# Leaving the next row out of the column steps of 32x32 triangular inverses, and doing it by itself

## The chip, the cores and the metric

The kernel runs on one core of one Trainium2 chip. The metric is the device time of one execution in microseconds (us), median of the runs. A core has several engines that each work through their own queue of instructions in order and wait for each other through semaphores: TensorE (PE in the profile; matrix products), VectorE (DVE), ScalarE (ACT), GpSimd (POOL), and SyncE (SP), which issues most of the DMA transfers.

## What is computed

Two blocks follow each other. The first is a delta-rule attention: for each of 4 x 8 heads, 768 tokens, head size 48, with normalised keys,

```
for t in range(S):
    y[t]  = q[t] @ state
    state = state + beta[t] * outer(k[t], v[t] - k[t] @ state)
```

The second sends each of the 3,072 resulting rows of 384 numbers to one of 16 experts (the best of 4 groups, then the best of 4 experts in it), each a two-layer network 384 -> 1024 -> 384 with a ReLU, scaled by the two gate probabilities. All is in fp32.

## The kernel before, in words

**Chunks.** The 768 tokens are cut into 24 chunks of C = 32. Within a chunk the recurrence is a triangular system: with the Gram matrix of the keys, a 32x32 unit lower triangular matrix per head is inverted, and then the whole chunk goes through TensorE. There are 128 partitions = 4 batches x 32 tokens, and after a transposition 128 partitions = 32 heads of four chunks; so one call of `inverse(g)` (lines 237 to 302) inverts the matrices of 4 chunks (RG = 4) at once, each partition holding a 32x32 matrix `m` of its own. Six such inverses serve the 24 chunks.

**An inverse.** `m` is transposed in from the Gram matrices `gt` (L243); a square root on ScalarE (L250) and some small VectorE operations give the norms and the scaling; two passes over 1,024 elements make `m` (L272) and `cs` (L277). Then come the column steps j = 1 .. 30. With n = 31 - j rows below row j, a step multiplies column j below row j by row j up to column j (`t`, n x j elements, L284) and adds the product to the block below row j (L288). Each of these operations reads what the one before it wrote. At the end come the product with `cs` (L290), the diagonal (L292), the transposition `mt` (L295) and, on ScalarE, two masked copies `mtb` (L300), which TensorE uses in the chunks.

**A chunk** (`advance(u)`, lines 315 to 370). TensorE brings in the scaled values `vh` (L321, made by VectorE at L308), subtracts what the state holds (L327) and starts the output (L336); ScalarE copies the result to `f`; TensorE applies the inverse (`w_ps`, L343); ScalarE copies to `w`; TensorE updates the state (`s_ps`, L353); ScalarE copies it to `s_bd` (L359), which the next chunk needs; TensorE finishes the output (L364). In between TensorE does the Gram products of a later chunk (`gram`, L225; ScalarE copies `gt`, VectorE masks `gq`, L233) and the router's logits of the chunk before (L385, L393; ScalarE's copy `lg`, L395).

**Routing** (`route(r)`, lines 398 to 497) takes the logits of four chunks: about 25 small VectorE operations find the group and the expert (`gb` L420 to `hots` L448), an exponential on ScalarE (L459), ranks `rk` from TensorE's `r_ps` (L462), `place` (L464), `mine` (L484); GpSimd compares (`at`, L489) and TensorE sorts (L495).

**The order** of TensorE, VectorE, ScalarE and GpSimd is written out by hand. VectorE's long tasks (inverses and routes) are generators that yield after each instruction, and a planner slips their instructions between the chunks' own: `work(n)` credits each running task with n x 180 x its share, and each instruction costs the task 180 plus the count of elements that it yields (`push`, line 507). Steps for ScalarE or TensorE wait for marked points in a chunk (`allow`). With `SHARE` = 0.9 the inverse of four chunks later is spread over about four chunks; inverse g starts when chunk 4(g-2)+2 ends, but its column steps do not begin before inverse g-1 is done.

**Then** the tokens are fetched by expert (GpSimd, L685) and the 16 experts run through TensorE (`hidden` L706, `second` L720), and results are scattered (L736).

Of the kernel before, what the change touches and what calls it, by code (L numbers as in the profile page):

```python
# [8 lines left out]
F32 = mybir.dt.float32  # L9
I32 = mybir.dt.int32  # L10
AX = mybir.AxisListType
ALU = mybir.AluOpType
# [3 lines left out]
C = 32  # L16
# [46 lines left out]
def deltanet_then_moe(  # L63
# [13 lines left out]
    nc = tc.nc  # L77
# [6 lines left out]
    NE, _, F = w1_d.shape  # L84
# [69 lines left out]
    with ExitStack() as first:  # L154
        ap_ = first.enter_context(tc.tile_pool(name="attn", bufs=1))
        wk = first.enter_context(tc.tile_pool(name="wk", bufs=2))
# [80 lines left out]
        def inverse(g):  # L237

            m = wk.tile([128, C, C], F32, tag="m", name=f"m{g}")
            flat = m.rearrange("p i j -> p (i j)")
            nc.vector.transpose(out=flat, in_=gts.pop(g).rearrange("p t u h -> p (t u h)"))  # L243
            yield C * C
            diag = flat[:, ::C + 1]
            nrm, r0, r1 = [sm.tile([128, C], F32, tag=n, name=f"{n}{g}")
                           for n in ("nrm", "r0", "r1")]
            nc.vector.tensor_tensor(r0, diag, cut["tiny"].to_broadcast([128, C]), op=ALU.max)
            yield ACT_STEP
            nc.scalar.activation(r0, r0, ACT.Sqrt)  # L250
            yield SOON
            nc.vector.reciprocal(r1, r0)
            yield
            nc.vector.tensor_tensor(r1, r1, diag, op=ALU.mult)
            yield
            nc.vector.tensor_tensor(r0, r0, r1, op=ALU.add)
            yield
            nc.vector.scalar_tensor_tensor(nrm, in0=r0, scalar=-0.5,
                                           in1=cut["eps"].to_broadcast([128, C]), op0=ALU.mult,
                                           op1=ALU.subtract)  # L260
            yield
            nc.vector.reciprocal(r1, nrm)
            yield
            nc.vector.tensor_tensor(r1, r1, r1, op=ALU.mult)
            yield
            nc.vector.scalar_tensor_tensor(r0, in0=r1, scalar=-1.0, in1=bt[:, g], op0=ALU.mult,
                                           op1=ALU.mult)
            yield
            norm[g] = sm.tile([128, C], F32, tag="normt", name=f"normt{g}")
            nc.vector.transpose(out=norm[g], in_=nrm)  # L270
            yield
            nc.vector.tensor_tensor(m, m, r0[:, :, None].to_broadcast([128, C, C]), op=ALU.mult)  # L272
            yield C * C
            while g and g - 1 not in mts:
                yield TURN
            cs = wk.tile([128, C, C], F32, tag="cs", name=f"cs{g}", bufs=1)
            nc.vector.tensor_tensor(cs, cut["below"].rearrange("p (i j) -> p i j", i=C),  # L277
                                    r0[:, None, :].to_broadcast([128, C, C]), op=ALU.mult)
            yield C * C
            for j in range(1, C - 1):  # L280
                n = C - 1 - j
                t = wk.tile([128, C * C // 4], F32, tag="t", name=f"t{g}_{j}")
                tv = t[:, 0:n * j].rearrange("p (i c) -> p i c", i=n)
                nc.vector.tensor_tensor(tv, m[:, j + 1:, j:j + 1].to_broadcast([128, n, j]),  # L284
                                        m[:, j:j + 1, 0:j].to_broadcast([128, n, j]),
                                        op=ALU.mult)
                yield n * j
                nc.vector.tensor_tensor(m[:, j + 1:, 0:j], m[:, j + 1:, 0:j], tv, op=ALU.add)  # L288
                yield n * j
            nc.vector.tensor_tensor(m, m, cs, op=ALU.mult)  # L290
            yield C * C
            nc.vector.tensor_scalar(diag, r0, -1.0, None, op0=ALU.mult)  # L292
            yield
            mt = wk.tile([128, RG * H, C], F32, tag="cs", name=f"mt{g}", bufs=1)
            nc.vector.transpose(out=mt.rearrange("p r i -> p i r"), in_=flat)  # L295
            mtb = wk.tile([128, RG * H, 2, C], F32, tag="mtb", name=f"mtb{g}")
            yield 2 * C * C
            yield ACT_STEP
            for a in range(2):
                nc.scalar.activation(mtb[:, :, a], mt, ACT.Copy,  # L300
                                     scale=cut["parity"][:, a:a + 1])
            mts[g] = mtb
# [198 lines left out]
        behind, held, rate, due = [], {}, {}, {}  # L501
# [5 lines left out]
        def push(task):  # L507
            said = next(task, "end")
            if said == "end":
                behind.remove(task)  # L510
                held.pop(task, None)
                allow(TURN)
            else:
                held[task] = said if isinstance(said, str) else None
                due[task] -= 180 + (said if isinstance(said, int) else 0)

        def work(n):


            for task in behind:  # L520
                due[task] = min(due[task] + n * 180 * rate[task], 4000.0)
            while True:
                able = [t for t in behind if held.get(t) is None and due[t] > 0]
                if not able:
                    break
                for task in able:
                    push(task)

        def allow(what):

            for task in list(behind):
                if held.get(task) is what:
                    push(task)
# [5 lines left out]
        with tc.manual_schedule(engines={mybir.EngineType.PE, mybir.EngineType.DVE,  # L539
# [4 lines left out]
            for u in range(RG):  # L544
# [3 lines left out]
                if u == 1:  # L548

                    nc.scalar.activation(kqt_[RG][:, 0, 0, 0:1], cut["tiny"], ACT.Copy)  # L550
                    load_rest()
            start(inverse(0), 1)
            for step in range(RG):
                work(6)
# [14 lines left out]
            nc.gpsimd.memset(acc[:, 0], 0.0)  # L569
            nc.gpsimd.tensor_copy(what[:, :, 0:2], cut["ids"].rearrange("p (u c) -> p u c", c=2))  # L570
            start(inverse(1), SHARE)
            for step in range(4):
                work(14)
# [5 lines left out]
            for u in range(NCH + 1):  # L579
# [27 lines left out]
                if u % RG == RG - 2 and u // RG + 2 < NGR:  # L607
                    start(inverse(u // RG + 2), SHARE)
# [9 lines left out]
            while behind:  # L618
# [16 lines left out]
                                           op1=ALU.add)  # L635
# [152 lines left out]
    with tc.For_i(0, n_over):  # L788
# [13 lines left out]
                                       op1=ALU.add)  # L802
# [9 lines left out]
                                op=ALU.mult)  # L812
# [5 lines left out]
        for u in range(NCH):  # L818
# [4 lines left out]
                None, op0=ALU.is_equal)  # L823
            nc.tensor.matmul(f_ps, lhsT=at, rhs=what[:, u], start=(u == 0), stop=(u == NCH - 1))
        by, rows = mp.tile([128, 1], F32, name="by"), mp.tile([128, 2], I32, name="rows")
# [57 lines left out]
```

## Time and profile before

The time is 583.0 us, the median of three runs (582.28 to 584.39). The profiled execution spans 586.5 us.

| | busy us | share | instructions |
|---|---|---|---|
| TensorE (PE) | 503.2 | 86% | 8166 |
| VectorE (DVE) | 251.1 | 43% | 751 |
| ScalarE (ACT) | 171.4 | 29% | 335 |
| GpSimd (POOL) | 105.2 | 18% | 110 |

How to read it: the page cuts the span into 40 equal slices, and a digit is an engine's busy share of a slice in tenths. A group's row names the line, engine and operation, what is written and read with the shapes, the count, the busy time and the mean ns of one, and the idle time before. A row of a timeline begins with the start and the duration in us; a bracket at its end gives the engine's idle time before it and what ended that. Instructions on VectorE may overlap, so the start of the next can lie before the end of the last.

Three stages can be told apart: up to 53 us the first inverse (TensorE has little to do), from 53 to 288 us the chunks, from 288 us the experts.

### The profile page before, as it was taken

What the parts mean: (1) busy time and instruction counts of PE and PEld (TensorE: products, weight loads), DVE (VectorE), ACT (ScalarE), POOL (GpSimd) and SP (SyncE); (2) the same over time, 40 slices, a digit from 0 to 9 for tenths busy, and PEclk for the clock granted to TensorE, in tenths of its full rate; (3) what the DMA queues carried; (4) which work ended last, traced back from release to release, by engine and by line L of the source; (5) the groups of instructions that cost most, each with busy time, mean ns of one, the idle gap of its engine ahead of it and who ended that gap; (6) DMA issues with size and microseconds to landing.
All of it is one profiled execution on the core that took longest, in us unless ns stands there. A gap on an engine that the chain in (4) does not pass through costs nothing.

```text
span 586.5 us, 18265 instructions
## 1 busy us (share of the span) xinstructions
PE 503.2 (86%) x8166; PEld 460.1 (78%) x8166; DVE 251.1 (43%) x751; ACT 171.4 (29%) x335; POOL 105.2 (18%) x110
## 2 busy tenths in 40 slices
PE   3213888988999979999599999999999999999993
PEld 2212667767777767778499999999999999999993
DVE  1788997989769879513441011111111111111110
ACT  2102345573564564543011121111111111111110
POOL 0000000002102121121334113414125222221111
PEclk9999998996979989899589999999999999999998
DMA  7990243432421222210126665666756666776400
GB/s 271 403 381 11 83 130 125 160 130 83 143 106 51 90 69 83 82 61 30 36 72 207 181 222 164 215 190 212 249 175 216 213 221 222 242 236 209 169 20 19
DMA packets 44321, 90.64 MB, mean 155 GB/s; under 512 B 9755, under 2 KB 29650, under 8 KB 44240
## 3 DMA queue, kind: packets, MB, share of 16 engines
q1 hardware_dynamic: 34256, 79.71, 40.0%
q0 software_dynamic: 9984, 9.74, 6.2%
q8 instruction: 65, 1.06, 0.8%
q14 instruction: 16, 0.13, 0.1%
HBM read 79.92 MB, written 9.66 MB: 153 GB/s over the span
## 4 chain that ended last, share of the span: by engine, by line
issue 33%; PE 23%; DVE 15%; POOL 12%; DMA 9%; ACT 6%; POOLq 0%; SPq 0%; ACTq 0%
DMA out_dram<-yo,to_i 8%; POOL xg L685 7%; POOL out_dram L736 5%; DVE t L284 4%; DVE m L288 4%; PE a_ps L321 3%; ACT s_bd L359 3%; PE w_ps L343 3%; PE s_ps L353 3%; PE a_ps L327 3%; PE o_ps L336 2%; PE g_ps L225 2%; PE s_ps L495 2%; PE t_ps L385 1%; DMA kqt<-in_kq_dram 1%
## 5 line engine op out<-in xcount | busy, mean ns | idle before, releaser
L706 PE MATMUL h_ps<-xt,w 128*128 128x224 f32 (+14 forms) x768 | 140.4, 337 | 0.6 <-DVE xt L697 0.6
L720 PE MATMUL y_ps<-hid,w 128*128 128x224 f32 (+14 forms) x768 | 138.8, 334 | 0.0
L706 PEld LDWEIGHTS h_ps<-xt,w 128*128 128x128 f32 x768 | 131.3, 192 | 1.6 <-DVE xt L697 0.9
L720 PEld LDWEIGHTS y_ps<-hid,w 128*128 128x128 f32 x768 | 129.3, 190 | 0.3
L697 DVE COPY xt<-t_ps 128x336 f32<-128x336 f32 (+14 forms) x32 | 15.1, 471 | 141.3 <-PE t_ps L695 141.3
L709 ACT ACTIVATE hid<-h_ps 128x448 f32<-128x448 f32 (+14 forms) x64 | 32.3, 505 | 126.9 <-PE h_ps L706 126.9
L735 DVE TENSOR_SCALAR yo<-o_ps,gate 112x384 f32<-112x384 f32 (+14 forms) x32 | 19.6, 616 | 106.3 <-PE o_ps L732 106.3
L284 DVE TENSOR_TENSOR t<-m 128x30 f32<-128x30 f32 (+9 forms) x180 | 60.3, 335 | 4.0
L288 DVE TENSOR_TENSOR m<-m,t 128x30 f32<-128x30 f32 (+9 forms) x180 | 60.0, 334 | 4.5
L685 POOL DMA_INDIRECT xg<-x_dram,from_i x32 | 39.2, 1225 | 115.8 <-PE t_ps L695 100.4
L736 POOL DMA_INDIRECT out_dram<-yo,to_i x32 | 39.2, 1225 | 101.9 <-DVE yo L735 101.0
L321 PE MATMUL a_ps<-vh,con 128*128 128x384 f32 x48 | 26.5, 639 | 33.3 <-DVE vh L308 21.8
L722 ACT ACTIVATE yt<-y_ps 128x224 f32<-128x224 f32 (+14 forms) x48 | 16.2, 338 | 120.2 <-PE y_ps L720 120.2
L359 ACT ACTIVATE s_bd<-s_ps 48x768 f32<-48x768 f32 x46 | 36.9, 803 | 17.6 <-PE s_ps L353 17.0
L321 PEld LDWEIGHTS a_ps<-vh,con 128*128 128x128 f32 x48 | 8.2, 214 | 36.5 <-DVE vh L308 19.9
L489 POOL TENSOR_SCALAR at<-con,place 128x256 f32<-128x256 f32 x20 | 19.9, 1001 | 89.7 <-DVE t L284 36.7
L450 POOL TENSOR_TENSOR acc<-acc,hots 128x16 f32<-128x16 f32 x20 | 5.7, 287 | 147.8 <-DVE hots L448 146.6
L343 PEld LDWEIGHTS w_ps<-f,mtb 64*64 64x64 f32 x768 | 25.6, 139 | 7.1 <-issue 4.9
L343 PE MATMUL w_ps<-f,mtb 64*64 64x48 f32 x768 | 28.9, 224 | 1.7 <-ACT f L331 1.1
L327 PEld LDWEIGHTS a_ps<-s_bd,kqt 128*32 128x32 f32 x736 | 18.1, 125 | 15.5 <-issue 15.5
L353 PE MATMUL s_ps<-w,kv 32*128 32x96 f32 x736 | 28.4, 293 | 0.5 <-issue 0.3
L353 PEld LDWEIGHTS s_ps<-w,kv 32*128 32x128 f32 x736 | 24.4, 198 | 3.1 <-issue 1.0
(115 smaller groups left out, 526.1 us busy)
## 6 DMA issues: line engine op xcount, KB each, us to landing
w<-in_w_dram SPq DMA_DIRECT2D x28, 1536.0 KB, 7.5
kqt<-in_kq_dram SPq DMA_DIRECT2D x24, 512.0 KB, 4.9
kv<-in_kv_dram SPq DMA_DIRECT2D x24, 448.0 KB, 3.4
x_dram<-x SPq DMA_DIRECT2D x24, 192.0 KB, 2.1
w<-in_w_dram SPq DMA_DIRECT2D x6, 512.0 KB, 9.6
w<-in_w_dram SPq DMA_DIRECT2D x4, 576.0 KB, 10.1
w<-in_w_dram SPq DMA_DIRECT2D x2, 384.0 KB, 9.6
con<-in_const_dram SPq DMA_DIRECT2D x1, 512.0 KB, 8.7
```

The costliest lines, as they stand in the source:

```text
L284: nc.vector.tensor_tensor(tv, m[:, j + 1:, j:j + 1].to_broadcast([128, n, j]), m[:, j:j + 1, 0:j].to_broadcast([128, n, j]), op=ALU.mult)
L288: nc.vector.tensor_tensor(m[:, j + 1:, 0:j], m[:, j + 1:, 0:j], tv, op=ALU.add)
L321: nc.tensor.matmul(a_ps.rearrange("p h d -> p (h d)"), lhsT=ident, rhs=vh.rearrange("p h d -> p (h d)"), start=True, stop=(u == 0), skip_g ...
L327: nc.tensor.matmul(a_ps[quads[b], 2 * j:2 * j + 2, :], lhsT=kqt[:, 0, j, quads[b]], rhs=s_bd[:, b, j], start=False, stop=True, skip_group_ ...
L343: nc.tensor.matmul(w_ps[b, h], lhsT=mt[b, uu * H + (h % 2) * NP + h // 2], rhs=f[b, h], start=True, stop=True, skip_group_check=True)
L353: nc.tensor.matmul(s_at[:, b, j], lhsT=k[quads[b], j], rhs=w[quads[b], 2 * j:2 * j + 2], start=(u == 0 and j == 0), stop=True, skip_group_ ...
L359: nc.scalar.activation(s_bd[rows, :, :, hh, :], s_at[rows, :, :, hh * D:(hh + 1) * D], ACT.Copy)
L685: nc.gpsimd.indirect_dma_start(out=xg[0:P, t, :], out_offset=None, in_=x_dram[:, :], in_offset=bass.IndirectOffsetOnAxis(ap=rows[0:P, t:t ...
L706: nc.tensor.matmul(h_ps[:, k], lhsT=w1[:, j, (f + k) * 128:(f + k + 1) * 128], rhs=xt[:, j], start=(j == 0), stop=(j == DC - 1), skip_grou ...
L709: nc.scalar.activation(hid[:, f:f + 2], h_ps, ACT.Relu)
L720: nc.tensor.matmul(y_ps, lhsT=w2[:, f, j * 128:(j + 1) * 128], rhs=hid[:, f], start=(f == 0), stop=(f == FC - 1))
L736: put = nc.gpsimd.indirect_dma_start(out=out[:, :], out_offset=bass.IndirectOffsetOnAxis(ap=to[0:P, i:i + 1], axis=0), in_=yo[:, :], in_of ...
```

## The change

Column step j leaves out row j+1, which is the row that step j+1 multiplies by; that row is done by itself in one `scalar_tensor_tensor` (`add_row`: row j times one number per partition, plus the row), between the product for the rows below it and their addition. So the addition no longer directly follows the product it reads, and the next step's product needs only the row, not the block written just before. Steps with one or two columns (j < 3) are done column by column in one instruction each (`add_column`), and those with at most two rows left (j = 29, 30) row by row. The scalar of these instructions is read from `m`, one number per partition. The planner's fixed cost of an instruction goes from 180 to 100.

The aim is that no VectorE operation reads what its neighbour wrote.

```diff
@@ inverse(g)
             for j in range(1, C - 1):
-                n = C - 1 - j
-                t = wk.tile([128, C * C // 4], F32, tag="t", name=f"t{g}_{j}")
-                tv = t[:, 0:n * j].rearrange("p (i c) -> p i c", i=n)
-                nc.vector.tensor_tensor(tv, m[:, j + 1:, j:j + 1].to_broadcast([128, n, j]),
-                                        m[:, j:j + 1, 0:j].to_broadcast([128, n, j]),
-                                        op=ALU.mult)
-                yield n * j
-                nc.vector.tensor_tensor(m[:, j + 1:, 0:j], m[:, j + 1:, 0:j], tv, op=ALU.add)
-                yield n * j
+            def add_column(j, c):
+                rows = m[:, j + 1:, c]
+                nc.vector.scalar_tensor_tensor(rows, in0=m[:, j + 1:, j], scalar=m[:, j, c:c + 1],
+                                               in1=rows, op0=ALU.mult, op1=ALU.add)
+            def add_row(j, i):
+                row = m[:, i, 0:j]
+                nc.vector.scalar_tensor_tensor(row, in0=m[:, j, 0:j], scalar=m[:, i, j:j + 1],
+                                               in1=row, op0=ALU.mult, op1=ALU.add)
+                n = C - 2 - j
+                if j < 3:
+                    for c in range(j):
+                        add_column(j, c)
+                        yield n + 1
+                elif n < 2:
+                    for i in range(j + 1, C):
+                        add_row(j, i)
+                        yield j
+                else:
+                    t = wk.tile([128, C * C // 4], F32, tag="t", name=f"t{g}_{j}")
+                    tv = t[:, 0:n * j].rearrange("p (i c) -> p i c", i=n)
+                    below = m[:, j + 2:, 0:j]
+                    nc.vector.tensor_tensor(tv, m[:, j + 2:, j:j + 1].to_broadcast([128, n, j]),
+                                            m[:, j:j + 1, 0:j].to_broadcast([128, n, j]),
+                                            op=ALU.mult)
+                    yield n * j
+                    add_row(j, j + 1)
+                    yield j
+                    nc.vector.tensor_tensor(below, below, tv, op=ALU.add)
+                    yield n * j
@@ push(task)
-                due[task] -= 180 + (said if isinstance(said, int) else 0)
+                due[task] -= 100 + (said if isinstance(said, int) else 0)
```

## The prediction

> **What bounds the kernel now.** I read the page's engine totals and slices first, then the stretches around each chunk, then the timelines of VectorE, TensorE and ScalarE where an engine waits.
>
> ```profile
> PE 503.2 (86%) x8166; PEld 460.1 (78%) x8166; DVE 251.1 (43%) x751; ACT 171.4 (29%) x335; POOL 105.2 (18%) x110
> PE   3213888988999979999599999999999999999993
> DVE  1788997989769879513441011111111111111110
> L284 DVE TENSOR_TENSOR t<-m 128x30 f32<-128x30 f32 (+9 forms) x180 | 60.3, 335 | 4.0
> L288 DVE TENSOR_TENSOR m<-m,t 128x30 f32<-128x30 f32 (+9 forms) x180 | 60.0, 334 | 4.5
> ```
>
> From 288 us to the end (298.5 us) the experts run: TensorE is busy 284.5 us of it, and the change touches nothing there. From 53 to 288 us the 24 chunks run, VectorE and TensorE both near full (161 and 169 us busy of the 190.6 up to 243.6). Before 53 us TensorE idles until VectorE has finished the first inverse. So the edited lines are on the end's path for sure only from 31 to 52 us; in the chunks it depends on who waits. VectorE's timeline:
>
> ```profile
> 22.00 0.42 DVE L233 TENSOR_TENSOR gq<-g_ps,con 128x256 f32<-128x256 f32 x1
> 22.33 0.19 DVE L284 TENSOR_TENSOR t<-m 128x30 f32<-128x30 f32 x1
> 22.55 0.21 DVE L288 TENSOR_TENSOR m<-m,t 128x30 f32<-128x30 f32 x1
> ...
> 30.83 0.42 DVE L233 TENSOR_TENSOR gq<-s_ps,con 128x256 f32<-128x256 f32 x1 [4.08 <-ACT gt L228]
> ...
> 49.28 1.22 DVE L290 TENSOR_TENSOR m<-m,cs 128x1024 f32<-128x1024 f32 x1
> ...
> 105.72 0.40 DVE L284 TENSOR_TENSOR t<-m 128x234 f32<-128x234 f32 x1
> 106.03 0.16 DVE L420 TENSOR_REDUCE gb<-lg 128x4 f32<-128x16 f32 x1
> 106.15 0.41 DVE L288 TENSOR_TENSOR m<-m,t 128x234 f32<-128x234 f32 x1
> 106.47 0.21 DVE L422 TENSOR_REDUCE eb<-lg 128x16 f32<-128x64 f32 x1
> 106.60 0.40 DVE L284 TENSOR_TENSOR t<-m 128x238 f32<-128x238 f32 x1
> ```
>
> (The 49.28 line ends the first inverse's steps.) Read two spacings. An instruction that needs nothing of its neighbour starts 0.08 us before the neighbour ends (22.00 to 22.33 behind 0.42). One that reads what the neighbour wrote starts 0.03 us after its end (22.33 to 22.55 behind 0.19). The dependence costs 0.11 us. The last five lines show what fills that bubble already: two routing operations stand between t and m, yet t to t is 0.88 us, as without them.
>
> ```profile
> L308 DVE TENSOR_TENSOR vh<-kv,normt 128x384 f32<-128x384 f32 x24 | 13.1, 547 | 0.0
> L735 DVE TENSOR_SCALAR yo<-o_ps,gate 112x384 f32<-112x384 f32 x4 | 2.5, 618 | 14.4 <-PE o_ps L732 14.4
> L697 DVE COPY xt<-t_ps 128x336 f32<-128x336 f32 x4 | 2.0, 507 | 15.1 <-PE t_ps L695 15.1
> ```
>
> These price the new form. PSUM as a source costs nothing extra (336 elements 507 ns, and 384 by the same slope 557), so the 618 of L735 holds some 60 ns for its scalar read per partition.
>
> ```profile
> 64.51 1.62 PE L321 MATMUL a_ps<-vh,con 128*128 128x384 f32 x2 [2.18 <-DVE vh L308]
> 132.02 0.55 PE L385 MATMUL t_ps<-con,x 128*128 128x128 f32 x3 [0.70 <-DVE rk L462]
> 135.09 1.06 PE L495 MATMUL s_ps<-mine,at 128*128 128x48 f32 x4 [1.45 <-DVE mine L484]
> ```
> ```profile
> 166.86 2.15 ACT L300 ACTIVATE mtb<-mt,con 128x1024 f32<-128x1024 f32 x2
> 169.01 1.28 ACT L250 ACT_TABLE_LOAD   x1
> 170.44 1.62 ACT L359 ACTIVATE s_bd<-s_ps 48x768 f32<-48x768 f32 x2
> ```
>
> In the chunks TensorE waits for VectorE only in such places: the first vh, and rk and mine of each route. Undisturbed chunks take 8.4 us (191.43 to 199.80 between the L321 starts), 7.7 without a gram. The longest ones are long for another reason too: in one chunk of four, mtb and the square root with its table load stand in ScalarE's queue ahead of s_bd, which the recurrence needs.
>
> [...]
>
> **The change, part by part.** (1) One inverse before: 60 operations, 9,920 elements: [...]. After: 26 triples (j=3..28), three operations for j=1, 2, three for j=29, 30; 84 in all, 32 of them scalar_tensor_tensor with a pointer scalar. In a triple the lower block needs the product t two places back, and t needs only the row step, so each starts 0.08 us early; but the row step takes a place: [...]. The triples hold 8,762+403 elements: [...] and the six ends, mostly still neighbours that wait, 1.5. Sum 18.6, so 3.0 saved. Bounds: if the pointer scalar is free, t still needs 0.11 us to reach the lower block, and I get 17.1 (4.5 saved); if nothing overlaps around it, 26 x 0.11 more, 21.5, nothing saved. I take the middle.
>
> (2) First inverse, on the path. Its gq of 30.83 us waits for ScalarE, which change and planner do not speed up. At 100 instead of 180 per operation the planner puts steps 8 to 10 ahead of that gq: they fall into the 4.08 us of idleness. What is left between 30.83 and the first vh (52.53), 21.7 us, loses those three (2.1) and some 2.1 by part 1 (18 steps by about 0.10, and the ends): vh at 48.4. **4.1 us saved**, and all after it moves up.
>
> (3) The chunks. I added up VectorE's order with these spacings, vh to vh, over one period of four chunks (u=8..11): before 5.4+8.6+8.3+9.9 = 32.2; after 7.8+8.3+9.5+7.3 = 33.0 (31.4 with a free scalar). So VectorE gains nothing here: the routing operations that stood free in the bubbles now cost their own time, and there are 24 more operations. It stays near the 33.5 of four undisturbed chunks. An edit of the inverse that saves 3 us alone saves none in company.
>
> (4) The planner's 100. Inverse 1 ends a chunk earlier, its mtb in chunk 2, its follower's root in chunk 3. Vh of chunk 1 comes 1.1 us later (11.3 of work ahead of it, not 10.2): +1.1, TensorE waits. Chunks 2 to 4: mtb alone holds ScalarE 2.15 us in chunk 2, instead of mtb and root with idle time in chunk 3: -1.4. Rk and mine of the routes come a chunk earlier, ahead of the next inverse's root instead of behind it: the 0.70 and 1.45 of chunk 8 and the slow TensorE clock after them (0.72 over 129 to 142 us) mostly go, but VectorE's backlog makes them about 0.4 and 0.7 late in chunk 7, and the exponential now precedes the root, so a table load of 1.28 joins mtb there: together chunks 7 to 10 -1.6. Periods 11 to 14 and 15 to 18 have their load already and pay the lateness of about 1.2: +0.4 and +0.6. Chunks 19 to 22: no such wait, -0.5. Sum -1.4. What waits behind a late rk on VectorE is vh, gq and the whole next inverse; for it, TensorE's t_ps, in order. The added exponential load has 1.45 us of ScalarE idleness ahead of f, which hides it. Tail and experts: 0, bound by TensorE.
>
> Sum: 583.0 - 4.1 - 1.4 = **577.5**.
>
> **Rivals.** A: the scalar costs less, VectorE's period falls to 31.4, rk and mine are on time: 4.5 per inverse, first stage -5.5, the four periods about -1.3 each more: some 571. For it: 32-element scalar_tensor_tensor with an immediate take 0.19. Against: L735. B: the chunks give the first stage back: the table load and the late rk of each period cost 1 us more than I allow, with clock loss behind: about 583, no change. C: pointer scalars break the overlap or cost 0.12: VectorE's period becomes about 35, over the 33.5; first stage -2, four periods at +2.5: 583 - 2 + 10 = 591, slower. For it: the trace never shows two such operations close together. Against: the 60 ns is seen on 32 of them.
>
> **Chances.** Mine 0.46, A 0.26, B 0.14, C 0.14. The range takes mine, A and B's middle and leaves out the far ends of A and C: 569 to 584.5. Within 0.5% is 580.1 to 585.9: B. Faster 0.72, same 0.14, slower 0.14.
>
> **What would show it.** The first vh near 48.4 us (else part 2); the row step near 0.23 us and the lower block 0.14 behind its start (part 1); vh to vh unchanged in sum, about 33 (part 3); a first chunk of 12, mtb in chunk 2, a table load before s_bd in chunk 7 (part 4). I am wrong if the chunks from first to last L321 (53.12 to 268.3, 215 us) change by more than 4 us either way.

## The result, and the profile after

The changed kernel takes 589.9 us (median of four runs, 588.91 to 591.76) against 582.8 before: a ratio of 1.0121, with a 95% interval of 1.0089 to 1.0153. It is slower by 7 us, where 577.5 was forecast. All medians leave out executions more than 1.5% above the kernel's fastest; with them two of the times below would be 582.8 instead of 581.9 us (price 116) and 579.6 instead of 577.8 (the last experiment). The page of the changed kernel (engine totals, slices, and the three main groups that stand for the two of before):

```profile
PE 502.6 (86%) x8166; PEld 459.1 (78%) x8166; DVE 246.6 (42%) x895; ACT 174.4 (30%) x337; POOL 106.8 (18%) x110
PE   3305989679879889999499999999999999999993
DVE  1799949949949859522441011111111111111110
...
L306 DVE TENSOR_TENSOR t<-m 128x81 f32<-128x81 f32 (+13 forms) x156 | 50.6, 325 | 0.2
L312 DVE TENSOR_TENSOR m<-m,t 128x81 f32<-128x81 f32 (+13 forms) x156 | 50.3, 323 | 0.0
L289 DVE SCALAR_TENSOR_TENSOR m<-m 128x29 f32<-128x29 f32 (+27 forms) x174 | 39.4, 229 | 0.4
```

Look at VectorE's slices: where the second to the sixteenth were between 6 and 9, a 4 or 5 now stands at every third (a slice is 14.7 us). VectorE has less to do and idles in a rhythm, while the time got longer. Its timeline in the first inverse:

```profile
29.65 0.42 DVE L233 TENSOR_TENSOR gq<-s_ps,con 128x256 f32<-128x256 f32 x1 [3.12 <-ACT gt L228]
...
34.32 0.39 DVE L306 TENSOR_TENSOR t<-m 128x224 f32<-128x224 f32 x1
34.63 0.23 DVE L289 SCALAR_TENSOR_TENSOR m<-m 128x16 f32<-128x16 f32 x1
34.77 0.38 DVE L312 TENSOR_TENSOR m<-m,t 128x224 f32<-128x224 f32 x1
35.08 0.38 DVE L306 TENSOR_TENSOR t<-m 128x221 f32<-128x221 f32 x1
...
43.32 1.23 DVE L314 TENSOR_TENSOR m<-m,cs 128x1024 f32<-128x1024 f32 x1
...
46.57 0.54 DVE L332 TENSOR_TENSOR vh<-kv,normt 128x384 f32<-128x384 f32 x1
```

Each of these operations starts about 0.08 us before its neighbour ends (34.63 against 34.32 + 0.39), and the row step of 0.23 us takes only 0.14 of a place. The first vh comes at 46.57 us, against 52.53. Where the gain is lost, on TensorE's timeline of the changed kernel:

```profile
59.44 1.62 PE L345 MATMUL a_ps<-vh,con 128*128 128x384 f32 x2 [3.07 <-DVE m L289]
117.69 0.69 PE L480 MATMUL r_ps<-hots,con 128*128 128x64 f32 x2 [4.15 <-DVE gq L233]
200.46 0.69 PE L480 MATMUL r_ps<-hots,con 128*128 128x64 f32 x2 [1.69 <-DVE gq L233]
```

The waits at rk and mine of before (3.6 us in all) are gone from chunks 7 to 18, and in their place TensorE stands at r_ps, before the next chunk may begin (6.1 us, with one of 0.26 that is not shown). It waits until VectorE has read a gq: the matmul results g_ps, t_ps and r_ps take turns in one PSUM buffer (`tag="g"` in the kernel), and gq is read from g_ps. VectorE around the 4.15 us, and just after:

```profile
115.47 1.91 DVE L319 STREAM_TRANSPOSE mt<-m 128x1024 f32<-128x1024 f32 x1
117.24 0.40 DVE L233 TENSOR_TENSOR gq<-g_ps,con 128x256 f32<-128x256 f32 x1
...
125.98 0.42 DVE L233 TENSOR_TENSOR gq<-g_ps,con 128x256 f32<-128x256 f32 x1 [4.81 <-ACT gt L228]
...
129.46 0.35 DVE L252 RECIPROCAL r<-r 128x32 f32<-128x32 f32 x1 [3.06 <-ACT r L250]
```

That gq stands behind the whole end of an inverse; less than ten microseconds later VectorE has nothing to do and waits twice. The two chunks as windows (length, then busy time and count of PE, PEld, DVE, ACT and POOL, the granted TensorE clock, and the share and GB/s of the DMA):

```profile
105.76:118.59 12.83, 8.55 (x271) 7.08 (x272) 12.66 (x46) 6.16 (x11) 1.69 (x4) 0.85 0.39 130
118.59:131.22 12.63, 9.52 (x273) 7.56 (x273) 4.32 (x20) 7.28 (x12) 2.96 (x3) 0.88 0.27 82
```

VectorE is busy 12.66 of 12.83 us, then 4.32 of 12.63. ScalarE in the second of them has the queue that was forecast:

```profile
125.74 2.15 ACT L324 ACTIVATE mtb<-mt,con 128x1024 f32<-128x1024 f32 x2
127.91 1.28 ACT L250 ACT_TABLE_LOAD   x1
...
129.34 1.62 ACT L383 ACTIVATE s_bd<-s_ps 48x768 f32<-48x768 f32 x2
```

A profile is one execution. That of before took 588.25 us, over its median, that of after 588.91, under its median, so their spans (586.5 and 587.1) differ by less than the medians do; I compare medians, and stages with this in mind. Read off the starts of the a_ps matmuls (L321 before) and of the first h_ps:

| profiled execution | start of chunk 0 | chunk 0 to 23 | of it TensorE busy, idle | 23 to experts | experts to end |
|---|---|---|---|---|---|
| before | 53.1 | 215.1 | 192.3, 22.8 | 25.9 | 292.4 |
| after | 47.2 | 223.2 | 193.2, 29.9 | 24.7 | 292.1 |
| new steps in the first inverse only | 46.9 | 210.1 | 187.2, 22.9 | 26.6 | 293.1 |
| new steps, inverses at 133, routes 180 | 47.1 | 212.2 | 190.1, 22.2 | 26.7 | 292.4 |
| old steps, 100 for all | 50.7 | 237.3 | 203.5, 33.8 | 24.9 | 292.8 |

All of the loss is in the chunks. All but 8 of their some 5,640 matmuls are the same in all five rows, so a longer busy time is slower matmuls, and a longer idle time is waits.

### The profile page after: what moved, and what is told of

The parts are those of the page before. It is cut to its first block, busy times and chain, and to the rows that moved or that the text cites. A ratio compares the mean times of both kernels' runs of the same rounds, so it can differ in the third digit from the quotient of the medians.

```text
span 587.1 us, 18412 instructions
## 1 busy us (share of the span) xinstructions
PE 502.6 (86%) x8166; PEld 459.1 (78%) x8166; DVE 246.6 (42%) x895; ACT 174.4 (30%) x337; POOL 106.8 (18%) x110
## 4 chain that ended last, share of the span: by engine, by line
issue 32%; DVE 30%; POOL 12%; PE 11%; DMA 9%; ACT 4%; POOLq 0%; SPq 0%; ACTq 0%
DMA out_dram<-yo,to_i 8%; POOL xg L709 7%; DVE t L306 7%; DVE m L312 6%; POOL out_dram L760 5%; DVE m L289 5%; DVE mt L319 2%; PE a_ps L345 2%; PE w_ps L367 2%; PE a_ps L351 1%; DVE m L314 1%; ACT mtb L324 1%; DVE vh L332 1%; DVE m L272 1%; DVE cs L277 1%
## 5 line engine op out<-in xcount | busy, mean ns | idle before, releaser
L306 DVE TENSOR_TENSOR t<-m 128x81 f32<-128x81 f32 (+13 forms) x156 | 50.6, 325 | 0.2
L312 DVE TENSOR_TENSOR m<-m,t 128x81 f32<-128x81 f32 (+13 forms) x156 | 50.3, 323 | 0.0
L289 DVE SCALAR_TENSOR_TENSOR m<-m 128x29 f32<-128x29 f32 (+27 forms) x174 | 39.4, 229 | 0.4
L474 POOL TENSOR_TENSOR acc<-acc,hots 128x16 f32<-128x16 f32 x20 | 7.3, 365 | 134.4 <-DVE m L289 88.1
```

The lines of the kernel that those rows point to most:

```text
L289: nc.vector.scalar_tensor_tensor(row, in0=m[:, j, 0:j], scalar=m[:, i, j:j + 1], in1=row, op0=ALU.mult, op1=ALU.add)
L306: nc.vector.tensor_tensor(tv, m[:, j + 2:, j:j + 1].to_broadcast([128, n, j]), m[:, j:j + 1, 0:j].to_broadcast([128, n, j]), op=ALU.mult)
L312: nc.vector.tensor_tensor(below, below, tv, op=ALU.add)
```

## The experiments

The change has two parts, the steps and the planner's price. Theory W: the price puts r_ps a chunk earlier, where it waits. Theory S: the new steps cost more where routing stands among them. Theory P (pace), a third: at 100 an instruction, the planner packs an inverse into VectorE's order faster than VectorE can work it off (a burst), and TensorE pays for the backlog wherever it next needs VectorE. Each ratio is to the kernel before, run beside it (medians of 582.7 to 583.5). In the experiments from the second on, but for the one that moves r_ps alone, each task has a price of its own (the second diff shows how); the later diffs, against the changed kernel, leave that part out.

**The price alone**, on the steps of before:

```diff
-                due[task] -= 180 + (said if isinstance(said, int) else 0)
+                due[task] -= 100 + (said if isinstance(said, int) else 0)
```

> The column steps of before with the planner's 100. Theory W (order): at 100 an instruction the route runs a chunk ahead, so TensorE's r_ps stands at the end of chunks 6, 10, 14 and 18 behind a gq that VectorE reaches only after the inverse's last operations; the loss is the planner's, so this kernel is slower than before, 586 to 596 us, with waits of 2 to 6 us at r_ps. Theory S (steps): the loss comes from the 24 more operations of each inverse, which this kernel does not have; then it is about 583 us or less.

606.2 us, ratio 1.0386 (1.0339 to 1.0433): 23 us slower, more than the 586 to 596 that W gave it. The price does harm by itself, on the old steps. Whether the new steps do harm as well, as S has it, this run can't tell.

**Routes back at 180**, all else as changed:

```diff
-                due[task] -= 100 + (said if isinstance(said, int) else 0)
+                due[task] -= price[task] + (said if isinstance(said, int) else 0)
-        def start(task, share):
+        def start(task, share, each=180):
...
+            price[task] = each
...
-            start(inverse(0), 1)
+            start(inverse(0), 1, 100)
...
-            start(inverse(1), SHARE)
+            start(inverse(1), SHARE, 100)
...
-                    start(inverse(u // RG + 2), SHARE)
+                    start(inverse(u // RG + 2), SHARE, 100)
```

> All of the change, but a route's instructions cost 180 in the planner as before (the inverses' still 100): r_ps is back at the end of chunks 7, 11, 15 and 19. Theory W: the waits at r_ps are gone, 575 to 581 us, faster than before by the 4 us of the first inverse and perhaps more. Theory S: the operations are all still there, 586 us or more. Theory P (pace: at 100 the inverse crowds VectorE's queue and gq comes late whatever the routes do): 583 to 590.

592.0 us, 1.0172 (1.0124 to 1.0221), five runs from 586.0 to 594.2. W falls: r_ps is back in its place, and the kernel is no faster than the changed one. P's 583 to 590 is a little too low. TensorE's timeline of this kernel, in the profiled execution, which is the fastest of the five:

```profile
117.81 0.55 PE L409 MATMUL t_ps<-con,x 128*128 128x128 f32 x3 [0.99 <-DVE gq L233]
...
131.99 1.04 PE L519 MATMUL s_ps<-mine,at 128*128 128x48 f32 x4 [1.45 <-DVE mine L508]
...
134.07 2.04 PE L377 MATMUL s_ps<-w,kv 32*128 32x96 f32 x32
...
177.07 0.61 PE L519 MATMUL s_ps<-mine,at 128*128 128x48 f32 x4 [1.42 <-DVE mine L508]
...
178.40 1.15 PE L377 MATMUL s_ps<-w,kv 32*128 32x96 f32 x32
```

The same gq holds t_ps now, then mine holds the sorting; after that wait the state's matmuls take 2.04 us, where they take 1.15 elsewhere. The 1.45 at mine and the 2.04 behind it stand in the profile of before too, so of the waits in this chunk only the 0.99 is new.

**Only r_ps moved** (and the exponential behind it), the prices left at 100:

```diff
             if n == RG:
                 yield NEXT
+                yield NEXT
```

> The changed kernel, but a route waits for one more chunk's start before r_ps and its exponential; nothing else of the planner is touched, r_ps stands at the end of chunks 7, 11, 15 and 19. Theory W: 576 to 582 us. Theory S: 586 or more. Theory P: 583 to 590.

592.0 us, 1.0141 (1.0073 to 1.021). W falls a second time. Its TensorE timeline:

```profile
119.11 0.55 PE L409 MATMUL t_ps<-con,x 128*128 128x128 f32 x3 [1.47 <-DVE gq L233]
...
130.18 0.55 PE L409 MATMUL t_ps<-con,x 128*128 128x128 f32 x3 [1.76 <-DVE rk L487]
...
133.24 0.62 PE L520 MATMUL s_ps<-mine,at 128*128 128x48 f32 x4 [1.45 <-DVE mine L509]
...
134.78 2.04 PE L377 MATMUL s_ps<-w,kv 32*128 32x96 f32 x32
```

In place of the 4.15 us stand 1.47, 1.76 and 1.45 at three other places, of which the kernel before had 0.70 at rk and the 1.45. The wait at r_ps is gone and the time has not come back, so that wait by itself was not the cause.

**The new steps in the first inverse alone**, at 100; the other five and the routes as before, at 180:

```diff
+            if g == 0:
...
+            else:
+                for j in range(1, C - 1):
+                    n = C - 1 - j
...
+            start(inverse(0), 1, 100)
...
+            start(inverse(1), SHARE, 180)
...
+                    start(inverse(u // RG + 2), SHARE, 180)
```

> The new steps in the first inverse alone, at 100 in the planner; the other five inverses and all routes as before, at 180. Both theories: the first vh comes 4 us earlier and the chunks are as before, 577 to 580 us. If it is not faster than before by 3 to 5 us, the gain of the first stage does not reach the end.

578.8 us, 0.9917 (0.9894 to 0.994): 4.5 us faster than its before of 583.3, as forecast for the first stage.

**All the new steps at the old pace**: inverses at 133, so that 84 instructions cost about what 60 did at 180; routes at 180.

```diff
+        def start(task, share, each=180):
...
+            start(inverse(1), SHARE, 133)
...
+                    start(inverse(u // RG + 2), SHARE, 133)
```

> All the new steps, but the planner paces them as it paced the old ones: 133 an instruction for the inverses (an inverse then takes about 4 chunks of credit again, not 3.5), 180 for the routes. Theory P (pace: at 100 the inverse is issued in a burst that VectorE cannot keep up with, and TensorE pays for the backlog wherever it next waits): 576 to 581 us. Theory S (the new steps cost more where routing operations stand among them): 584 to 592 us, well above the 578.8 of the run with the new steps in the first inverse alone.

579.3 us, 0.9933 (0.9902 to 0.9965). Against the kernel with inverses at 100 (592.0) only this number differs, and it is worth over 12 us. S falls as the cause of the loss: with the old steps in the five later inverses it was 578.8, with overlapping intervals. P's forecast came true. How the price becomes time is another matter: in the chunks of the two profiles (218.7 and 212.2 us) TensorE idles 23.6 and 22.2 us, and is busy 195.1 and 190.1.

**The routes at 100**, inverses at 133:

```diff
+        def start(task, share, each=100):
...
+            start(inverse(1), SHARE, 133)
...
+                    start(inverse(u // RG + 2), SHARE, 133)
```

> All the new steps, inverses at 133, routes at 100, so r_ps is again at the end of chunks 6, 10, 14, 18. Theory P: 577 to 583 us, since the inverses are not in a burst. Theory W (the place of r_ps): 584 to 590. Theory S: 584 to 592.

581.0 us, 0.995 (0.9927 to 0.9972). Here r_ps stands at the ends of chunks 6, 10, 14 and 18 again, and TensorE's trace has no wait at r_ps; it has some at rk:

```profile
109.35 0.43 PE L480 MATMUL r_ps<-hots,con 128*128 128x64 f32 x2
...
113.89 0.55 PE L409 MATMUL t_ps<-con,x 128*128 128x128 f32 x3 [1.66 <-DVE rk L486]
```

With the inverses at 133, W's place costs little: 581.0 against 579.3, with intervals that overlap.

**The old steps with the burst**: inverses at 100, routes at 180.

```diff
             for j in range(1, C - 1):
-                n = C - 2 - j
...
+                n = C - 1 - j
...
+        def start(task, share, each=180):
...
+            start(inverse(0), 1, 180)
...
+            start(inverse(1), SHARE, 100)
...
+                    start(inverse(u // RG + 2), SHARE, 100)
```

> The steps of before, inverses at 100, routes at 180. Theory P: an inverse is issued in 3.3 chunks instead of 4.1, so most of the 23 us that 100 for all cost with the old steps are here too: 592 to 606 us. Theory W: those 23 us came with the routes: 580 to 586 us.

599.5 us, 1.0264 (1.023 to 1.0298). Of the 23 us of the first experiment 16 come with the price of the five later inverses. The other 7 come with that of the routes and of the first inverse, so on the old steps the routes' price does harm too.

**Two more prices**, all new steps, routes at 180; first 116:

```diff
+        def start(task, share, each=180):
...
+            start(inverse(1), SHARE, 116)
...
+                    start(inverse(u // RG + 2), SHARE, 116)
```

> All the new steps, inverses at 116, routes at 180: between the kernels with 100 (592.0) and 133 (579.3), an inverse in 3.8 chunks of credit. Theory P (pace): between the two, 581 to 588 us, TensorE's waits for VectorE too. If it is not the pace but one accident of the order at 100, it is at 579 like 133.

581.9 us, 0.998 (0.9955 to 1.0005). Then 145, the same lines with that number:

```diff
+            start(inverse(1), SHARE, 145)
...
+                    start(inverse(u // RG + 2), SHARE, 145)
```

> All the new steps, inverses at 145, routes at 180: an inverse in 4.25 chunks of credit. Theory P: no burst, 577 to 582 us; it grows again only where mt comes too late for the chunk that needs it.

576.9 us, 0.9898 (0.9841 to 0.9956). The chunks with an inverse's end, as windows of this kernel:

```profile
110.59:120.68 10.09, 7.92 (x271) 6.70 (x272) 7.66 (x19) 6.47 (x12) 0.00 (x0) 0.95 0.42 143
120.68:131.85 11.17, 10.88 (x271) 8.62 (x272) 11.09 (x45) 5.82 (x11) 2.88 (x3) 0.74 0.28 83
```

VectorE has 7.7 and 11.1 us of work in chunks of 10.1 and 11.2, not 12.7 in the one and 4.3 in the other. Slow matmuls are not gone from this kernel: in the second chunk TensorE is busy for 10.9 us, at a granted clock of 0.74.

**Slower still**:

```diff
+        def start(task, share, each=180):
...
+            start(inverse(1), SHARE, 160)
...
+                    start(inverse(u // RG + 2), SHARE, 160)
```

> All the new steps, inverses at 160, routes at 180: an inverse in 4.45 chunks of credit, so each begins a little before the one before has ended. Theory P: the trend of 592.0, 582.8, 579.3, 576.9 (at 100, 116, 133, 145) flattens or turns here, 574 to 580 us; it turns where mt comes so late that the chunk which needs it waits.

583.9 us, 1.0004 (0.9979 to 1.0029), above the 574 to 580 expected: it turns. TensorE's timeline (the profile puts the second wait down to an m that ended in the 0.15 us between the end of mine and the matmuls):

```profile
206.04 0.55 PE L409 MATMUL t_ps<-con,x 128*128 128x128 f32 x3 [2.15 <-DVE rk L486]
...
209.06 1.06 PE L519 MATMUL s_ps<-mine,at 128*128 128x48 f32 x4 [1.41 <-DVE m L289]
```

It is not mt that comes too late, as I expected, but rk and mine again: with each inverse longer in the queue, its end and the next one's steps stand in front of the route. So the price has a best place: 592.0, 581.9, 579.3, 576.9, 583.9 at 100, 116, 133, 145, 160. It lies between 116 and 160; the intervals at 133 and 145 overlap.

**The new steps where no routing runs beside them** (inverses 0 and 1, at 100 and 133), the old ones at 180 elsewhere:

```diff
+            if g < 2:
...
+            else:
+                for j in range(1, C - 1):
+                    n = C - 1 - j
...
+            start(inverse(0), 1, 100)
...
+            start(inverse(1), SHARE, 133)
...
+                    start(inverse(u // RG + 2), SHARE, 180)
```

> The new steps in the two inverses that have no routing operations beside them (0 at 100, 1 at 133), the old ones in the other four at 180. Theory S and the tally: another 1 to 3 us below the run with the first inverse alone, 576 to 578 us, if the second inverse is on the path; theory P has no view beyond 576 to 580.

577.2 us, 0.9867 (0.9829 to 0.9905), 1.6 below the new steps in the first inverse alone, with intervals that overlap.

**The same with the slower pace**, 145 and 197:

```diff
+            start(inverse(1), SHARE, 145)
...
+                    start(inverse(u // RG + 2), SHARE, 197)
```

> The new steps in inverses 0 (at 100) and 1 (at 145), the old ones in the other four, at 197 instead of 180 (about 4.3 chunks of credit), routes at 180. If only the pace counts and the new steps bring nothing where routes run beside them, this is as fast as the best kernel with new steps everywhere: 574 to 578 us. If the new steps help there too, it stays at the 577.2 of the same kernel at 180 or above.

577.8 us, 0.9896 (0.9855 to 0.9937), runs from 573 to 581. This one is inconclusive: the intervals of this kernel, of the one before it and of the new steps everywhere at 145 overlap. Whether the new steps in the four inverses beside routes bring anything at all can't be told from the times. The kernel of the experiment before this one and the kernel at 145 are faster than both kernels of this case.

## Why the prediction was wrong, point by point

**Part 1, the steps, was right.** What an operation takes for its count of elements was my estimate, and the profile of before bears it out: t takes 194 ns with 30 elements and 405 with 240 (L284 by shape), about 1.0 ns an element, and the 60 operations of an inverse are busy 20.05 us ((60.3 + 60.0)/6) and, each 0.03 after the last, take an estimated 21.9, where I had 18.6 + 3.0. A triple with 224 elements takes 35.08 - 34.32 = 0.76 us; two operations of 0.39 us that each start 0.08 early, and the 0.14 forecast for the row step, make 0.76. The first inverse, from 20.35 us (its first column step) to 43.32, less 3.12 of idleness and five gq at 0.33, takes 18.2 us where I had estimated 18.6. The price of the scalar, taken from another operation, held too. A PSUM source showed no cost of its own before (gq, 256 elements from g_ps, 419 ns, at the 1.0 ns of t an estimated 421), and the slope used is that of the COPY rows of L697 before (252 elements 420 ns, 336 elements 507: 1.04 ns an element). In the groups by shape of the changed kernel stand

```profile
L289 DVE SCALAR_TENSOR_TENSOR m<-m 128x27 f32<-128x27 f32 x6 | 1.4, 234 | 0.0
...
L289 DVE SCALAR_TENSOR_TENSOR m<-m 128x3 f32<-128x3 f32 x6 | 1.3, 215 | 0.0
...
L266 DVE SCALAR_TENSOR_TENSOR r<-r,bt 128x32 f32<-128x32 f32 x6 | 1.1, 192 | 0.2
```

L266 has an immediate as its scalar, L289 one number per partition. At the 1.0 ns an element of t, the 234 and the 215 are 47 and 52 ns above the 192, so some 50 ns are the scalar's here. And the next operation does start early behind the row step: at 34.77, 0.09 us before its end.

**Part 2, the first inverse, was right**: 4.1 us forecast; the first vh came 6.0 us earlier, of which 1.65 is this execution's earlier start (the pass over m at L272 at 17.75 us, not 19.40); alone, it measured 4.5 us to the end.

**Part 3, VectorE gains little in company, was right in kind**, with the size off. From vh 8 to vh 12 on VectorE's timeline, idle times taken off, the profile of before has 34.5 us of work (34.1 with the new steps in the first inverse only) and the changed one 33.7: 0.8 less, where I worked out 0.8 more. The changed kernel's period was near what I had (33.0); that of before, which its own profile already showed, I had 2.3 too short (32.2). From vh 0 to vh 4, without routes, it is 34.9 and 31.7. The same steps save 3 us alone and under 1 beside a route, whose operations already stood in the bubbles.

**Part 4, the planner, is the step that failed.** It said -1.4 us for the chunks. By the profiles, chunks 0 and 1 lost 0.5 where I had +1.1; chunks 2 to 5 gained 0.1 (-1.4); 6 to 10, which takes in one chunk more than my 7 to 10, lost 4.8 (-1.6); 11 to 14 lost 2.3 (+0.4); 15 to 18 lost 1.9 (+0.6); 19 to 22 gained 1.3 (-0.5): +8.1 in all. Against the profile with the old order behind the new first inverse it is 223.2 - 210.1 = 13.1, which is near what the medians say: 589.9 - 578.8 = 11.1.

The error was in what I compared. I added VectorE's work over a period, 33.0 us (the four terms give 32.9), set it against 33.5 of four undisturbed chunks, and called it near enough. The sum came out, and the time did not: what counts is where the work stands, and which engine waits behind it. The table's second and third stretches, 8.3 and 9.5 us (measured 8.2 and 9.3), meet chunks that take 7.8 us here (97.95 to 105.76), so VectorE is behind when gq comes; then the root of the next inverse is queued behind mtb on ScalarE and VectorE idles. Idle time on VectorE between vh 8 and vh 12 is 7.9 us in the changed kernel and 2.6 in the one with new steps in the first inverse only. I priced the lateness at 0.4 and 0.7 us for rk and mine, and did not see that r_ps, moved to the end of chunk 6, cannot start before a gq frees its buffer. But the two kernels with r_ps moved back show that finding that wait would not have been enough: the price of the inverses is the cause, shown by the row of prices with the same instructions in it.

That it acts as a burst, as theory P has it, fits, but is not shown by itself. How evenly the work lies does not tell the kernels apart: between vh 8 and vh 12 VectorE has, stretch by stretch, 5.7, 9.2, 8.5 and 11.1 us of work before, 8.2, 8.2, 9.3 and 8.0 in the changed kernel, and 8.2, 8.4, 8.1 and 8.9 at 145.

My rival B, that the chunks give the first stage back, was the nearest and too small: it had 1 us a period from a table load and a late rk. The table load (1.28 us at 114.32 in the changed kernel) hardly is the cause: the kernel with inverses at 133 and routes at 100 has its r_ps, and with it the exponential, in the same chunks, and takes 581.0; that its exponential brought the load was not shown. Rival C was right in its side only; pointer scalars did not break the overlap (0.14 us from the row step to its neighbour). The sign I set myself, chunks changed by over 4 us, is met.

The way from late work to lost time is known in part. Of the 13.1 us between those two profiles 7.0 are idle time of TensorE (29.9 against 22.9), in about equal parts waits for VectorE (9.8 against 6.7) and for ScalarE (16.9 against 13.4). The other 6 are the same matmuls taking longer (193.2 against 187.2 us busy; the mean granted clock of the two executions is 0.952 and 0.958, and 0.92 in the chunks of the changed kernel), where I had the slow matmuls of chunk 8 mostly go. No run holds the clock and changes the waits, so whether the waits bring the slow matmuls is open. The clock alone is not the cause: executions with a mean granted clock of 0.952 take 588.9 to 590.0 us in the changed kernel, and 579.0 and 584.3 us at 116.

## What to carry to other kernels

Removing the bubbles between dependent operations saved 3 us over four chunks where no route ran beside the inverse, and under 1 where a route's operations already stood in them: count what a planner already interleaves before removing a dependence. When a change makes tasks of more, shorter instructions, a planner's price per instruction is part of the change; keep the sum of a task's price, and so its pace, and test the two parts apart (with the same instructions it was 592.0 us at 100 and 579.3 at 133). VectorE's work summed over a period said little about the time (33.7 us against 34.5 before, and the chunks took 8.1 longer), and how evenly it was spread said little more: ask behind which piece of work another engine waits. And removing the longest wait of a trace need not bring its time back: with the 4.15 us at r_ps the time was 589.9, without them 592.0.

## What had not been expected of the hardware

A scalar_tensor_tensor with a scalar per partition took VectorE some 50 ns longer here (27 elements 234 ns, against 192 for 32 elements with an immediate), but it overlaps its neighbours: the row step at 34.63 us starts 0.08 before the operation ahead of it ends, and the next one 0.09 before its own end, so its place in this chain is 0.14 us, not the 0.23 of its row. A wait of some 1.4 us on TensorE can be followed by many slow matmuls or by none, in one kernel: with the routes at 180, the 32 matmuls of s_ps take 2.04 us after the wait of 1.45 at 131.99 and 1.15 us after the wait of 1.42 at 177.07. The slow ones need not come at once: where only r_ps was moved, the sorting itself takes 0.62 us after its wait of 1.45 at 133.24, and the s_ps behind it 2.04. No run tells what decides that.
